# A block of cluster attention, token mixer and feed-forward: the value product in narrower column tiles, the weight conversions laid elsewhere in the queues

## The chip, the cores and the metric

The kernel runs on one core of one Trainium2 chip. What is measured is the device time of one execution in microseconds, the median of several runs. Names used below: PE is TensorE (matrix products), DVE is VectorE, ACT is ScalarE, POOL is GpSimd, SP is the engine whose queue issues the loads and stores.

## The reference

What is computed, with B = 2 batches, 8 heads, 768 tokens, 64 dimensions a head, 512 channels:

```python
q_assign = np.argmax(np.einsum('bhsd,hcd->bhsc', q_n, c_n), axis=-1)   # 16 clusters
k_assign = np.argmax(np.einsum('bhsd,hcd->bhsc', k_n, c_n), axis=-1)
mask = q_assign[:, :, :, None] == k_assign[:, :, None, :]
scores = np.where(mask, scale * np.matmul(q, k.transpose(0, 1, 3, 2)), -1000000000.0)
attn = softmax(scores)                                # rows, 1e-9 added to the sum
x = np.matmul(attn, v)                                # heads side by side: (B, S, 512)

theta = x @ w_theta                                   # token mixer
y = w_tok_r @ (x * cos(theta)) + w_tok_i @ (x * sin(theta))
x = x + y
x = x + np.maximum(x @ w_ch, 0.0)                     # channel mix

u = x + ((x.transpose(0, 2, 1) @ U) @ V).transpose(0, 2, 1)   # rank 32 over tokens
out = u + np.maximum(u @ w_ch1, 0.0) @ w_ch2          # feed-forward, 2048 wide
```

(The softmax is written out in the reference; the last three products are float32 too.)

## The kernel before

Everything works on tiles of 128 partitions. The order of each engine's instructions is the order in which the program is written (a manual schedule); an engine whose next instruction waits holds up all behind it.

**Products in parts.** A float32 operand is often split into a high part (rounded, written by ACT: `wh`, `xh`, `uh`, `z`, `gh`) and a low part (the rest, written by POOL or DVE: `wl`, `xl`, `ul`, `gl`). A product is then three passes: high with high, high with low, low with high (`PASSES`).

**Attention.** Eight groups g, each two heads of one batch. A group has six steps p. In each step PE computes a pair of key tiles' scores for one head (`scores_pair`, L301), ACT their exponentials `p` (L306); PE also computes the next group's row maxima (`max_pair`, L249). The value product `pv` (L314) is queued by pairs of key tile kt and half of the queries hf, and taken off in the odd steps, four pairs at a time. In step 5, and in step 1 of the next group, the row sums (`sum_keys`, L333) stand directly ahead of such a value block; they multiply with a block of ones into four tiles of 32 columns. After each step `fill` gives a number of units of other work to DVE, ACT and POOL: first the queue `bg`, then pieces of conversions.

**Conversions.** The weights are stored in 64 bits and have to be turned into float32. One `Convert` covers 768 columns: load 768 KB into one of two stage buffers `st`, then `magnitude` (ACT, L382, tile `cv`), `bits` (DVE, L386), `top` (DVE, L390), `low` (DVE, L394), then the high part `wh` (ACT, L399) and the low part `wl` (POOL, L403). `conv_step` issues the next piece; after `low` it puts the two last ones into `conv_after` and starts the next load (`conv_start` loads only while fewer than two conversions are in work). `conv_until` and `wcol` issue all pieces that are still missing when PE's program comes to a product that needs the tile. The order of the conversions is one queue: w_theta, then w_tok_r and w_tok_i by turns, then w_ch, then w_ch1 (`w1`) and w_ch2 (`w2`) with U and V (`ub`, `vs`) among them.

**Token mixer.** 24 steps (u, st), 26 with the lead of two. Step n computes theta on PE (L476, L480), then a chain ACT L483, DVE L484 and L485, ACT L486 to L488, DVE L493, ACT L496 gives z = x cos, x sin in high parts; the low parts are L502, the first on DVE, the second on POOL. `ymix` (L518) for step n - 2 follows on PE: 24 matrix products of 384 columns. Three `conv_step` stand in each step, except that steps 16 to 19 have one. From step 20, POOL computes `xl` (`split_x`, L463) for the channel mix.

**Channel mix to feed-forward.** `chmix(b, e)` (L536, 24 products of 384 columns) writes x back with two additions on DVE (L541); `turn` transposes it in four pieces (L552). `low1` (L588) and `low2` (L608, additions L610) are the rank-32 part. `split_u` (L615, L616) makes `uh` and `ul`. Then 48 pairs (c, f) of the feed-forward: `ff1(c, f)` (L633, results `gh` L638 and `gl` L640) runs two ahead of `ff2(c, f)` (L653). ff1(c, f) uses columns 512 f to 512 f + 511 of w1's row of tiles, so f = 0 lies in its first tile of 768 columns, f = 3 in the third.

Of the kernel before, what the change touches and what calls it, by code (L numbers as in the profile page):

```python
# [10 lines left out]
F32 = mybir.dt.float32  # L11
# [9 lines left out]
B, H, S, D, C = 2, 8, 768, 64, 16  # L21
DM, RANK, DFF = 512, 32, 2048
P = 128
# [17 lines left out]
def tile_cluster_block(ctx: ExitStack, tc: tile.TileContext, qk, v, cent, wth, wr, wi, wch,  # L41
# [9 lines left out]
    def slot(name, dt=F32, shape=None):  # L51
        return sp.tile(shape or [P, S], dt, tag="slot", name=name)
# [57 lines left out]
    def cols(hf):  # L110
        return slice(hf * HALF, (hf + 1) * HALF)
# [198 lines left out]
    def pv(g, kt, hf):  # L310
        if kt == 0 and hf == 0:
            pvt[g] = banks("pv", "pv")
        for h in range(2):
            nc.tensor.matmul(out=pvt[g][hf][64 * h:64 * h + 64, :HALF], lhsT=v_t[g][:, kt, 64 * h:64 * h + 64],  # L314
                             rhs=pt[g, h, kt][:, hf * HALF:(hf + 1) * HALF],
                             start=(kt == 0), stop=(kt == NT - 1))

    def pv_out(g):
# [235 lines left out]
    ub = []  # L554
    vs = []

    def keep_u0(c):
        for i in range(4):
            t = slot(f"ub{i}", F32, [P, 6, P])
            nc.gpsimd.memset(t, 0.0)  # L560
            ub.append(t)

    def keep_u(c, g):
        z = c.t.rearrange("p (k r) -> p k r", r=RANK)
# [130 lines left out]
    def attention():  # L695
# [12 lines left out]
        for g in range(NG):  # L708
# [13 lines left out]
            if g == 2:  # L722
                tok = [c for p in zip(weigh_in(wr, NT * S, wr_t), weigh_in(wi, NT * S, wi_t)) for c in p]
                conv_load.extend(tok[:6])
                late = tok[6:]
            if g == 6:
                conv_load.extend(late)
# [5 lines left out]
            for p in range(NT):  # L733
# [24 lines left out]
                if g > 0 and p == 5:  # L758
                    bg.appendleft((.95, lambda: norm_x(g - 1)))
                    bg.appendleft((.97, lambda: spread(g - 1)))  # L760
                fill(1.7 if nxt else 3.4)
                if g > 0 and p == 1:
                    max_rows(g, 1)
                if nxt and p == 3:
# [105 lines left out]
    def mixer():  # L870
# [4 lines left out]
        for n in range(len(seq) + LEAD):  # L875
            if n < len(seq):
                theta(*seq[n])
                conv_step()
                theta_z(*seq[n])
            if n >= LEAD:  # L880
                ymix(*seq[n - LEAD])
            if n == 1:
                row_sums(last)
            if n == 2:
                spread(last)
                norm_x(last)
            if n not in range(16, 20):
                conv_step()
            if n < len(seq):
                theta_lo(*seq[n])  # L890
            if n not in range(16, 20):
                conv_step(1)
            if n in (9, 10):
                for t in range(2):
                    split_x(1, 2 * (n - 9) + t)
            if n == 12:
                conv_load.extend(weigh_in(wch, NP * DM, wch_t))
                c1, c2 = weigh_in(w1, NF * DM, w1_t), weigh_in(w2, NF * DM, w2_t)
                conv_load.extend([c1[0], c2[0]])
                conv_load.append(Convert(u_in, S, 0, [keep_u0] + [lambda c, g=g: keep_u(c, g) for g in range(4)], 32, 4))  # L900
                conv_load.append(Convert(v_in, S, 0, [keep_v, keep_vl], 32))
                for p in zip(c1[1:], c2[1:]):
                    conv_load.extend(p)
                conv_start()
            if 20 <= n <= 23:
                split_x(0, n - 20, nc.gpsimd)
            if n in (24, 25):
                split_x(1, n - 24, nc.gpsimd)

        for e in range(NP):  # L910
            chmix(0, e)
            if e in (0, 1):
                split_x(1, 2 + e)
            turn(0, e)
            conv_step()
        conv_until(uv, "u")
        conv_until(uv, "v")
        chmix(1, 0)
        turn(1, 0)
        low1(0)  # L920
        conv_step()
        chmix(1, 1)
        turn(1, 1)
        conv_step()
        low2(0, 0)
        low2(0, 1)
        split_u(0, 0)
# [82 lines left out]
```

## Time and profile before

| what | value |
|---|---|
| median of 3 runs (lowest to highest) | 720.88 us (719.17 to 721.48) |
| the profiled execution | 724.71 us, span 722.9 us |
| TensorE (PE) busy | 695.8 us, 96% of the span |
| VectorE (DVE), ScalarE (ACT), GpSimd (POOL) busy | 435.8, 300.9, 198.0 us |
| mean granted TensorE clock | 0.986 |

The span is the time from the first to the last instruction of the profiled execution. Attention ends at about 254.7 us of it, the mixer at 404.3, the feed-forward begins at 444.4. A granted clock of 1.00 is TensorE's full speed. Time in which an engine that is not the bottleneck stands idle costs nothing, so what counts is what PE waits for, and in which stage.

### The profile page before, as it was taken

The numbers are of one execution on the slowest core, as the hardware profiler recorded it, in microseconds if no ns is written. First come the engines' busy times: TensorE is split into PE (matmuls) and PEld (weight loads), VectorE is DVE, ScalarE is ACT, GpSimd is POOL, SyncE is SP. The second block draws the span as 40 slices with busy tenths as digits, with TensorE's granted clock in tenths as the row PEclk, the third lists the DMA queues.
The fourth block names the chain that finished last, engine by engine and source line by source line (L and its number), as shares of the span: only waits on it lengthen the run. The fifth ranks groups of instructions, "written<-read, shape, count | busy, mean of one in ns | idle before, by whom it ended". The sixth has DMA issues, their size and how long they took to land.

```text
span 722.9 us, 10608 instructions
## 1 busy us (share of the span) xinstructions
PE 695.8 (96%) x4109; PEld 550.2 (76%) x4110; DVE 435.8 (60%) x746; ACT 300.9 (42%) x613; POOL 198.0 (27%) x191
## 2 busy tenths in 40 slices
PE   7689998999999999999996999999999999999997
PEld 3455554665655499999995999898888888888986
DVE  5786996888898553448587877635344453332222
ACT  5654754665677634445464612422222222110000
POOL 9603224144155521113254712321221211100000
PEclk9899999999999999999999899999999999999999
DMA  7968667576422500002122211022122221100112
GB/s 216 224 141 246 175 154 200 168 178 155 127 88 88 175 1 1 2 1 73 44 55 88 88 44 44 0 88 88 45 87 58 74 87 30 30 1 0 59 40 77
DMA packets 21506, 64.05 MB, mean 89 GB/s; under 512 B 4272, under 2 KB 6192, under 8 KB 21456
## 3 DMA queue, kind: packets, MB, share of 16 engines
q1 hardware_dynamic: 21456, 63.37, 30.6%
q8 instruction: 32, 0.52, 0.3%
q14 instruction: 18, 0.15, 0.1%
HBM read 40.94 MB, written 3.15 MB: 61 GB/s over the span
## 4 chain that ended last, share of the span: by engine, by line
PE 84%; DVE 8%; ACT 4%; DMA 2%; issue 1%; SPq 0%; DVEq 0%; ACTq 0%
PE g L633 19%; PE acc L653 18%; PE y L518 11%; PE st L301 8%; PE pv L314 8%; PE h L536 5%; PE l L333 4%; PE th L476 4%; PE smax L249 4%; DVE mx L253 3%; PE h L588 1%; DMA st<-in_wr_dram 1%; DVE tht L484 1%; PE sims L119 1%; ACT p L306 1%
## 5 line engine op out<-in xcount | busy, mean ns | idle before, releaser
L403 POOL TENSOR_TENSOR wl<-cv,wh 128x768 fp32r<-128x768 f32 (+1 forms) x40 | 80.3, 2008 | 228.5 <-ACT wh L399 171.8
L640 DVE SCALAR_TENSOR_TENSOR gl<-g,gh 128x512 fp32r<-128x512 f32 x48 | 33.2, 692 | 155.7 <-ACT gh L638 155.7
L638 ACT ACTIVATE gh<-g 128x512 fp32r<-128x512 f32 x48 | 28.7, 598 | 202.1 <-PE g L633 202.1
L253 DVE TENSOR_REDUCE mx<-smax 128x1 f32<-128x512 f32 x144 | 90.1, 681 | 29.8 <-PE smax L249 29.5
L518 PE MATMUL y<-wh,z 128*128 128x384 f32 x384 | 89.9, 346 | 6.9 <-ACT z L496 6.9
L306 ACT ACTIVATE p<-st 128x512 f32<-128x512 f32 x192 | 79.2, 505 | 33.6 <-PE st L301 27.0
L633 PE MATMUL g<-uh,wh 128*128 128x512 f32 (+1 forms) x256 | 87.0, 340 | 0.0
L633 PE MATMUL g<-uh,wl 128*128 128x512 f32 (+1 forms) x256 | 86.6, 338 | 0.0
L633 PE MATMUL g<-ul,wh 128*128 128x512 f32 (+1 forms) x256 | 86.2, 337 | 0.0
L301 PE MATMUL st<-qp,kp 128*128 128x256 f32 (+1 forms) x384 | 80.8, 354 | 1.1 <-ACT p L306 1.1
L653 PE MATMUL acc<-gh,wh 128*128 128x512 f32 x192 | 76.0, 396 | 0.0
L653 PE MATMUL acc<-gh,wl 128*128 128x512 f32 x192 | 75.6, 394 | 0.0
L653 PE MATMUL acc<-gl,wh 128*128 128x512 f32 x192 | 75.4, 393 | 0.0
L518 PEld LDWEIGHTS y<-wh,z 128*128 128x128 f32 x384 | 68.2, 192 | 7.8 <-ACT z L496 7.7
L301 PEld LDWEIGHTS st<-qp,kp 128*128 128x128 f32 x384 | 58.2, 194 | 19.1 <-issue 6.1
L314 PE MATMUL pv<-p,v 128*64 128x384 f32 x384 | 67.7, 496 | 2.2 <-ACT p L306 2.1
L314 PEld LDWEIGHTS pv<-p,v 128*64 128x64 f32 x384 | 25.5, 137 | 40.3 <-issue 33.4
L633 PEld LDWEIGHTS g<-ul,wh 128*128 128x128 f32 x256 | 48.5, 190 | 6.5 <-POOL ul L616 0.4
L633 PEld LDWEIGHTS g<-uh,wl 128*128 128x128 f32 x256 | 48.5, 189 | 5.7
L633 PEld LDWEIGHTS g<-uh,wh 128*128 128x128 f32 x256 | 48.4, 189 | 5.6
L518 PE MATMUL y<-wl,z 128*128 128x384 f32 x192 | 49.7, 340 | 0.0
L502 POOL TENSOR_TENSOR z<-tht,z 128x256 fp32r<-128x256 f32 x24 | 19.7, 821 | 94.8 <-ACT z L496 94.7
(129 smaller groups left out, 1206.4 us busy)
## 6 DMA issues: line engine op xcount, KB each, us to landing
st<-in_w_dram SPq DMA_DIRECT2D x20, 768.0 KB, 4.2
raw<-in_qk_dram SPq DMA_DIRECT2D x16, 384.0 KB, 5.3
qp<-hi SPq DMA_DIRECT2D x30, 192.0 KB, 2.9
st<-in_wr_dram SPq DMA_DIRECT2D x6, 768.0 KB, 4.5
st<-in_wi_dram SPq DMA_DIRECT2D x6, 768.0 KB, 4.3
kp<-hi SPq DMA_DIRECT2D x32, 96.0 KB, 2.9
qp<-lo SPq DMA_DIRECT2D x32, 96.0 KB, 2.7
v<-in_v_dram SPq DMA_DIRECT2D x8, 384.0 KB, 4.9
```

The costliest lines, as they stand in the source:

```text
L249: nc.tensor.matmul(out=ps[:, c:c + w], lhsT=qp[s, h, 0][:, (a + j) * P:(a + j + 1) * P], rhs=kp[s, h, 0][:, k0:k0 + w], start=True, stop=True)
L253: nc.vector.tensor_reduce(mx_t[g, h][:, o:o + n], ps.rearrange("p (n w) -> p n w", n=n), axis=AX.X, op=ALU.max)
L301: nc.tensor.matmul(out=ps[:, c:c + n], lhsT=kp[s, h, w][:, (a + j) * P:(a + j + 1) * P], rhs=qp[s, h, w][:, q0:q0 + n], start=(w == 0), st ...
L306: nc.scalar.activation(out=pt[g, h, a + j][:, q0:q0 + n], in_=ps[:, c:c + n], func=AF.Exp, scale=float(D) ** -0.5)
L314: nc.tensor.matmul(out=pvt[g][hf][64 * h:64 * h + 64, :HALF], lhsT=v_t[g][:, kt, 64 * h:64 * h + 64], rhs=pt[g, h, kt][:, hf * HALF:(hf + ...
L333: nc.tensor.matmul(out=ps[o:o + 32, :HALF], lhsT=ones, rhs=pt[g, h, kt][:, cols(hf)], start=(kt == 3 * a), stop=(kt == 3 * a + 2))
L403: nc.gpsimd.tensor_tensor(t[:, :c.w], c.t, f32(c.hi[:, :c.w]), op=ALU.subtract)
L518: nc.tensor.matmul(out=yps[u, j][hf][:, :HALF], lhsT=lhs, rhs=w[st][e][:, hf * HALF:(hf + 1) * HALF], start=(st == 0 and n == 0), stop=(st ...
L536: nc.tensor.matmul(out=ps[hf][:, :HALF], lhsT=wv[a], rhs=xs[b, t][c][:, hf * HALF:(hf + 1) * HALF], start=(n == 0), stop=(n == 11))
L633: nc.tensor.matmul(out=ps[:, o:o + w], lhsT=wv[a], rhs=us[b, t][e][:, s0:s0 + w], start=(n == 0), stop=(n == 11))
L640: nc.vector.scalar_tensor_tensor(gl, ps, 0.0, f32(gh), op0=ALU.max, op1=ALU.subtract)
L653: nc.tensor.matmul(out=aps[c, e], lhsT=wv[a], rhs=g[x], start=(first and i == 0), stop=(last and i == 2))
```

## The change

The value product is written in four tiles of 32 columns for each (kt, hf), in place of two of 64. The loads are asked for as soon as the first token weights are queued in group 2. In group 7, `fill` gets 2.0 units a step in place of 3.4. In the mixer, steps 16 and later have no conversion pieces; `split_x(0, .)` goes from POOL to DVE; the clearing of `ub` goes from U's conversion to steps 13 to 16, one tile each. w1 and w2 come after U and V in the queue. In the channel mix three pieces, and later two, stand where one stood.

```diff
@@ -310,9 +310,9 @@
     def pv(g, kt, hf):
         if kt == 0 and hf == 0:
             pvt[g] = banks("pv", "pv")
-        for h in range(2):
-            nc.tensor.matmul(out=pvt[g][hf][64 * h:64 * h + 64, :HALF], lhsT=v_t[g][:, kt, 64 * h:64 * h + 64],
-                             rhs=pt[g, h, kt][:, hf * HALF:(hf + 1) * HALF],
+        for r in range(0, P, 32):
+            nc.tensor.matmul(out=pvt[g][hf][r:r + 32, :HALF], lhsT=v_t[g][:, kt, r:r + 32],
+                             rhs=pt[g, r // 64, kt][:, cols(hf)],
                              start=(kt == 0), stop=(kt == NT - 1))
 
     def pv_out(g):
@@ -554,11 +554,10 @@
     ub = []
     vs = []
 
-    def keep_u0(c):
-        for i in range(4):
-            t = slot(f"ub{i}", F32, [P, 6, P])
-            nc.gpsimd.memset(t, 0.0)
-            ub.append(t)
+    def clear_u(i):
+        t = slot(f"ub{i}", F32, [P, 6, P])
+        nc.gpsimd.memset(t, 0.0)
+        ub.append(t)
 
     def keep_u(c, g):
         z = c.t.rearrange("p (k r) -> p k r", r=RANK)
@@ -722,6 +721,7 @@
             if g == 2:
                 tok = [c for p in zip(weigh_in(wr, NT * S, wr_t), weigh_in(wi, NT * S, wi_t)) for c in p]
                 conv_load.extend(tok[:6])
+                conv_start()
                 late = tok[6:]
             if g == 6:
                 conv_load.extend(late)
@@ -758,7 +758,7 @@
                 if g > 0 and p == 5:
                     bg.appendleft((.95, lambda: norm_x(g - 1)))
                     bg.appendleft((.97, lambda: spread(g - 1)))
-                fill(1.7 if nxt else 3.4)
+                fill(1.7 if nxt else 2.)
                 if g > 0 and p == 1:
                     max_rows(g, 1)
                 if nxt and p == 3:
@@ -875,7 +875,8 @@
         for n in range(len(seq) + LEAD):
             if n < len(seq):
                 theta(*seq[n])
-                conv_step()
+                if n < 16:
+                    conv_step()
                 theta_z(*seq[n])
             if n >= LEAD:
                 ymix(*seq[n - LEAD])
@@ -884,26 +885,27 @@
             if n == 2:
                 spread(last)
                 norm_x(last)
-            if n not in range(16, 20):
+            if n < 16:
                 conv_step()
             if n < len(seq):
                 theta_lo(*seq[n])
-            if n not in range(16, 20):
-                conv_step(1)
+            if n < 16:
+                conv_step()
             if n in (9, 10):
                 for t in range(2):
                     split_x(1, 2 * (n - 9) + t)
             if n == 12:
                 conv_load.extend(weigh_in(wch, NP * DM, wch_t))
                 c1, c2 = weigh_in(w1, NF * DM, w1_t), weigh_in(w2, NF * DM, w2_t)
-                conv_load.extend([c1[0], c2[0]])
-                conv_load.append(Convert(u_in, S, 0, [keep_u0] + [lambda c, g=g: keep_u(c, g) for g in range(4)], 32, 4))
+                conv_load.append(Convert(u_in, S, 0, [lambda c, g=g: keep_u(c, g) for g in range(4)], 32, 4))
                 conv_load.append(Convert(v_in, S, 0, [keep_v, keep_vl], 32))
-                for p in zip(c1[1:], c2[1:]):
+                for p in zip(c1, c2):
                     conv_load.extend(p)
                 conv_start()
+            if 13 <= n <= 16:
+                clear_u(n - 13)
             if 20 <= n <= 23:
-                split_x(0, n - 20, nc.gpsimd)
+                split_x(0, n - 20)
             if n in (24, 25):
                 split_x(1, n - 24, nc.gpsimd)
 
@@ -912,16 +914,16 @@
             if e in (0, 1):
                 split_x(1, 2 + e)
             turn(0, e)
-            conv_step()
+            conv_step(3)
         conv_until(uv, "u")
         conv_until(uv, "v")
         chmix(1, 0)
         turn(1, 0)
         low1(0)
-        conv_step()
+        conv_step(2)
         chmix(1, 1)
         turn(1, 1)
-        conv_step()
+        conv_step(2)
         low2(0, 0)
         low2(0, 1)
         split_u(0, 0)
```

DVE at the start of the feed-forward. `ul12` is the low part of u for the second batch's third tile, `cv_4675` and `cv_4980` (before) are w1's and w2's fourth tiles, `cv_4877` (changed) w1's third tile and `cv_5134` w2's third; `gl` are the feed-forward's low parts. Before:

```order
L616 TENSOR_TENSOR ul12_4936<-xT6_2850,uh12_4935 128x768
L640 SCALAR_TENSOR_TENSOR gl_4974<-g_4959,gh_4972 128x512
L390 SCALAR_TENSOR_TENSOR cv_4675<-st_4532,cv_4675 128x768
L394 SCALAR_TENSOR_TENSOR cv_4675<-st_4532,cv_4675 128x768
L640 SCALAR_TENSOR_TENSOR gl_5023<-g_4996,gh_5021 128x512
L386 TENSOR_SCALAR cv_4980<-cv_4980 128x768
```

Changed:

```order
L615 TENSOR_TENSOR ul12_5103<-xT6_3006,uh12_5102 128x768
L386 TENSOR_SCALAR cv_4877<-cv_4877 128x768
L390 SCALAR_TENSOR_TENSOR cv_4877<-st_4836,cv_4877 128x768
L394 SCALAR_TENSOR_TENSOR cv_4877<-st_4836,cv_4877 128x768
L386 TENSOR_SCALAR cv_5134<-cv_5134 128x768
L390 SCALAR_TENSOR_TENSOR cv_5134<-st_4879,cv_5134 128x768
L639 SCALAR_TENSOR_TENSOR gl_5158<-g_5126,gh_5156 128x512
```

All three pieces of w1's third tile now stand between `ul12` and the low part `gl_5158` of the result of ff1(0,3), which reads that tile; before, it had been converted in the channel mix.

POOL at the mixer's start. `z` are the low parts of x sin of the first steps, `rl` the last group's reciprocal row sums, `wl` low parts of token weights. Before:

```order
L403 TENSOR_TENSOR wl_2882<-cv_2854,wh_2880 128x768
L502 TENSOR_TENSOR z_2989<-tht_2979,z_2989 128x256
L349 COPY rl_3023<-rl4_3020 32x12 x8
L502 TENSOR_TENSOR z_3018<-tht_3008,z_3018 128x256
L502 TENSOR_TENSOR z_3059<-tht_3049,z_3059 128x256
```

Changed:

```order
L502 TENSOR_TENSOR z_3170<-tht_3157,z_3170 128x256
L403 TENSOR_TENSOR wl_3177<-cv_3011,wh_3172 128x768
L349 COPY rl_3211<-rl4_3208 32x12 x8
L502 TENSOR_TENSOR z_3206<-tht_3195,z_3206 128x256
L403 TENSOR_TENSOR wl_3224<-cv_3165,wh_3220 128x768
L502 TENSOR_TENSOR z_3251<-tht_3241,z_3251 128x256
```

A low part of a token weight now stands ahead of the copies of `rl` and of the second step's `z`, another ahead of the third's.

DVE around turn(0,3), whose four transposes of `xT3` are the last that low1(0) waits for. `cv_4530` (before) is w2's third tile; `cv_4663` and `cv_4710` (changed) are w1's and w2's first, `vs` belongs to V. Before:

```order
L552 STREAM_TRANSPOSE xt2_4484<-xT2_1596 128x6x32
L552 STREAM_TRANSPOSE xt3_4485<-xT2_1596 128x6x32
L386 TENSOR_SCALAR cv_4530<-cv_4530 128x768
L541 SCALAR_TENSOR_TENSOR xT3_1939<-h_4569,xT3_1939 128x384
L541 SCALAR_TENSOR_TENSOR xT3_1939<-h_4570,xT3_1939 128x384
L552 STREAM_TRANSPOSE xt0_4482<-xT3_1939 128x6x32
L552 STREAM_TRANSPOSE xt1_4483<-xT3_1939 128x6x32
L552 STREAM_TRANSPOSE xt2_4484<-xT3_1939 128x6x32
L552 STREAM_TRANSPOSE xt3_4485<-xT3_1939 128x6x32
L390 SCALAR_TENSOR_TENSOR cv_4530<-st_4441,cv_4530 128x768
```

Changed:

```order
L552 STREAM_TRANSPOSE xt3_4602<-xT2_1668 128x6x32
L577 TENSOR_TENSOR vs_4672<-cv_4608,vs_4672 32x768
L394 SCALAR_TENSOR_TENSOR cv_4663<-st_4610,cv_4663 128x768
L386 TENSOR_SCALAR cv_4710<-cv_4710 128x768
L390 SCALAR_TENSOR_TENSOR cv_4710<-st_4665,cv_4710 128x768
L541 SCALAR_TENSOR_TENSOR xT3_2035<-h_4720,xT3_2035 128x384
L541 SCALAR_TENSOR_TENSOR xT3_2035<-h_4721,xT3_2035 128x384
L552 STREAM_TRANSPOSE xt0_4599<-xT3_2035 128x6x32
L552 STREAM_TRANSPOSE xt1_4600<-xT3_2035 128x6x32
L552 STREAM_TRANSPOSE xt2_4601<-xT3_2035 128x6x32
L552 STREAM_TRANSPOSE xt3_4602<-xT3_2035 128x6x32
L394 SCALAR_TENSOR_TENSOR cv_4710<-st_4665,cv_4710 128x768
```

Where one piece stood between two turns, there are now three, and the low part of V.

## Rows read from the trace of the kernel before

**Rows 1.** The page: busy time, share of the span and instructions of each engine.

```profile
PE 695.8 (96%) x4109; PEld 550.2 (76%) x4110; DVE 435.8 (60%) x746; ACT 300.9 (42%) x613; POOL 198.0 (27%) x191
```

**Rows 2.** Windows: us, length, busy time of PE, PEld, DVE, ACT, POOL; clock, DMA, GB/s.

```profile
112.40:115.90 3.50, 3.50 (x13) 2.09 (x10) 0.84 (x1) 0.79 (x2) 1.70 (x1) 0.51 0.84 316
...
270.00:360.00 90.00, 90.00 (x593) 90.00 (x592) 47.61 (x89) 43.40 (x107) 18.05 (x19) 1.00 0.08 24
...
360.00:405.00 45.00, 38.43 (x225) 37.70 (x224) 36.44 (x43) 27.46 (x61) 22.02 (x16) 0.92 0.25 75
...
395.70:402.60 6.90, 5.01 (x16) 5.01 (x17) 4.70 (x7) 6.77 (x16) 1.69 (x2) 0.51 0.37 113
```

**Rows 3.** Chain of waits in the attention: start us, us, engine, result, line, instructions.

```profile
120.20 2.07 PE l L333 x24
...
122.27 2.73 PE pv L314 x16
...
244.69 7.89 PE pv L314 x48
```

**Rows 4.** Timeline of PE, group 7: start, us, instruction, idle before and releaser.

```profile
239.73 1.77 PE L301 MATMUL st<-qp,kp 128*128 128x512 f32 x8 [1.11 <-ACT p L306]
...
241.87 2.82 PE L333 MATMUL l<-p,ones 128*32 128x384 f32 x24 [0.38 <-ACT xT L321]
```

**Rows 5.** Timeline of ACT, group 7.

```profile
238.30 0.90 ACT L382 ACTIVATE cv<-st 128x768 f32<-128x768 f32 x1 [3.44 <-DMA st<-in_wr_dram]
```

**Rows 6.** Timelines of POOL and PE at the mixer's start.

```profile
266.30 0.74 POOL L502 TENSOR_TENSOR z<-tht,z 128x256 fp32r<-128x256 f32 x1
...
266.00 0.59 PE L518 MATMUL y<-wh,z 128*128 128x384 f32 x2
```

**Rows 7.** Chain of waits at the mixer's end and in the channel mix.

```profile
397.59 6.72 PE y L518 x24
...
404.31 20.82 PE h L536 x120
```

**Rows 8.** Timelines of DVE and POOL in the mixer's last steps.

```profile
380.78 4.64 DVE L484 TENSOR_SCALAR tht<-tht 128x256 f32<-128x256 f32 x1
...
382.50 2.78 POOL L560 MEMSET ub<- 128x768 f32 x4
```

**Rows 9.** Timeline of DVE in the channel mix.

```profile
403.13 2.06 DVE L525 TENSOR_TENSOR xT<-y,xT 128x384 f32<-128x384 f32 x4
...
405.11 2.45 DVE L394 SCALAR_TENSOR_TENSOR cv<-st,cv 128x768 int32<-128x768 int32 x1
...
421.65 1.01 DVE L541 SCALAR_TENSOR_TENSOR xT<-h,xT 128x384 f32<-128x384 f32 x2
...
422.58 1.14 DVE L552 STREAM_TRANSPOSE xt<-xT 128x192 f32<-128x192 f32 x4
...
443.79 0.96 DVE L616 TENSOR_TENSOR ul<-xT,uh 128x768 fp32r<-128x768 f32 x1
```

**Rows 10.** Chain of waits at the feed-forward's start.

```profile
462.40 2.77 PE g L633 x12
```

**Rows 11.** Timeline of DVE at the feed-forward's start.

```profile
462.65 0.96 DVE L616 TENSOR_TENSOR ul<-xT,uh 128x768 fp32r<-128x768 f32 x1
...
466.45 1.65 DVE L390 SCALAR_TENSOR_TENSOR cv<-st,cv 128x768 int32<-128x768 int32 x1
...
468.14 0.96 DVE L394 SCALAR_TENSOR_TENSOR cv<-st,cv 128x768 int32<-128x768 int32 x1
...
472.15 0.55 DVE L386 TENSOR_SCALAR cv<-cv 128x768 int32<-128x768 int32 x1
```

**Rows 12.** Timeline of POOL at the feed-forward's start.

```profile
463.62 1.84 POOL L616 TENSOR_TENSOR ul<-xT,uh 128x768 fp32r<-128x768 f32 x1 [2.09 <-ACT uh L615]
...
465.42 1.86 POOL L403 TENSOR_TENSOR wl<-cv,wh 128x768 fp32r<-128x768 f32 x1
```

**Rows 13.** Timeline of ACT at the feed-forward's start.

```profile
471.40 0.84 ACT L399 ACTIVATE wh<-cv 128x768 fp32r<-128x768 f32 x1
```

## The prediction

> **What bounds the kernel now.** I read the shares first: TensorE (PE) is busy for 695.8 us of a span of 722.9 us [rows 1], so every gain must come out of the 27 us in which it stands idle, or out of passes that it runs too slowly. Next come the windows: from 270 to 360 us PE is busy for 90.00 of 90.00 us, though every step of the token mixer there has conversion pieces beside it; from 360 to 405 us it is busy for 38.43 of 45.00 us, and in 395.70 to 402.60 us the granted clock is 0.51 [rows 2]. That is the lower of its two levels, 1.2 GHz for 2.4. Then the chain of waits and the timelines say what PE waits for. Three places matter: group 7 of the attention, the mixer's last steps, and the passage from the channel mix into the feed-forward, where PE hardly waits at present.
>
> **The change part by part.** All costs are set against the profiled execution (724.71 us, span 722.9). It lies 3.83 us above the median of the three runs, 720.88; I carry the difference over to the median.
>
> *The value product.* One pair (kt, hf) is now two passes of two 64-column tiles each; it becomes two passes of four 32-column tiles each. The same shape is there already in the row sums: 24 instructions, six passes, take 2.07 us, 0.345 a pass; 16 value instructions, eight passes, take 2.73 us, 0.341 a pass [rows 3]. So a pass of four narrow tiles is no faster than one of two wide ones. What can go is the step from one tile shape to the other. The last value block, 24 passes in a row, takes 7.89 us, 0.329 a pass [rows 3]; by this 2.73 us hold 0.10 us beyond the eight passes. A value block follows row sums directly at 15 places: 15 x 0.10 = **-1.5 us**. Bounds: -1.9, were it 0.125 each, and +0.7, were each of the 192 passes to take the 0.004 us more that separates 0.345 from 0.341.
>
> The Trainium skill, "TensorEngine Tiling (Array Packing)", section Theoretical Speedup, gives up to 2x for a free dimension of up to 64 and up to 4x for up to 32; by it the change would halve the value blocks. Rival D takes this up.
>
> *The added start of loads in group 2.* It finds two conversions already loaded and does nothing: the queue that issues loads (SP) reads alike through the attention in both orders. The wait for a token-weight load in that group, with the slow clock behind it at 112.4 us [rows 2], stays. **0.**
>
> *Less filling in group 7.* Two token-weight conversions fewer lie in the last group. There ScalarE (ACT) stood 3.44 us before a load [rows 5] while the exponentials queued behind it; PE waited 1.11 and 0.38 us, and the row sums took 2.82 instead of 2.07 us [rows 3, 4]. The changed order has the conversion that waited one step later, when its load has had that much longer. 1.11 + 0.38 + 0.75 = **-2.2 us** (bounds 0, if the later conversion waits as long, and -2.2).
>
> *The two conversions in the mixer's first steps.* They now lie in the chain of theta(0) and theta(1). On VectorE (DVE) a 0.55 us and a 0.95 us piece stand ahead of theta(1)'s first operation; a third, 0.96, lies where DVE waits for ACT's sines anyway. On GpSimd (POOL) a low half of 1.85 us stands ahead of eight copies and of z's low half. That low half ran from 266.30 for 0.74 us, and y(1), begun at 266.00, reads it after ten of its 24 instructions, at 266.00 + 10/24 x 4.16 = 267.73 [rows 6]: 0.69 us of slack. Alone, 1.5 us on DVE cost 1.5 - 0.69 = 0.8 us. If one DVE operation must also wait for the 1.85 us on POOL, 2.65. I take **+1.7 us** in the middle.
>
> *No conversions after step 15, clearing of ub spread, split_x on DVE.* Between 360 and 405 us PE idles for 45.00 - 38.43 = 6.57 us [rows 2]. The last y takes 6.72 us [rows 7] where 24 instructions of the same width take 20.82 / 5 = 4.16: 2.55 us for the low clock after the longest wait. What PE waits for is DVE and ACT: one operation on DVE, 0.30 us alone, took 4.64 us while POOL went from a split to four clearings without a break [rows 8]. All of these leave the place. From 270 to 360 us PE never waits with more work beside it [rows 2], so I give the whole back: 6.57 + 2.55 = **-9.1 us** (bounds -6.6, the idle time alone, and -9.1).
>
> *What these steps did must be done elsewhere.* Channel weight tile 2 is finished on demand in chmix(0,0): its low half on POOL comes about when the fourth quarter wants it, **+0.3 us** (0 to 0.7).
>
> Then the channel mix. In the order, DVE goes from the mixer's last additions (2.06 us, begun at 403.13, 1.2 us ahead of chmix [rows 7, 9]) through four pairs of additions of 1.01, four turns of 1.14, two splits of 0.96 [rows 9, 11], a small one that I put at 0.7, a narrower piece of about 0.64 (two thirds of 0.96), three rounds of 0.55 + 0.95 + 0.96 and a last 0.55 + 0.95 [rows 11], to the end of turn(0,3). This sums to 22.8 us (2.06 + 4.04 + 4.56 + 1.92 + 0.7 + 0.64 + 7.38 + 1.5), so it ends 21.6 us after chmix begins. low1(0) wants it 20.82 us [rows 7] + 0.3 after that. Before, the same turn ended at 422.58 + 1.14 = 423.72 [rows 9] and low1 began at 404.31 + 20.82 = 425.13: 1.4 us of slack become -0.5. And pieces there run long beside POOL: one took 2.45 us that takes 0.96 alone [rows 9, 11], 1.5 more. Bounds 0.5, with no piece hit, and 5.0, with three; I take one: **+2.0 us**. Behind it ff1(0,0) wants ul02, which was ready at 443.79 + 0.96 = 444.75 [rows 9], hardly in time. Two more pieces, 0.95 + 0.96, stand ahead of it on DVE: **+1.5 us** (0 to 1.9).
>
> *The first feed-forward tiles.* This is the largest cost. ff1(0,3) reads the third tile of w1. Before, that tile was ready, and ff1(0,3) began at 462.40 without a wait [rows 10]. In the changed order its conversion is forced at that point: DVE does its three pieces behind ul12, ACT its high half, POOL its low half, and PE stands. I lay this on the rows of before. ul12 ends on DVE at 462.65 + 0.96 = 463.61; the first piece, 0.55, ends at 464.16. POOL is in ul13 to 463.62 + 1.84 = 465.46, and a low half of w2 follows at once, 1.85, to 467.31 [rows 11, 12]. Before, a piece that is 0.95 alone took 1.65 us at 466.45 and ended when POOL's 1.86 us did, give or take 0.95 [rows 11, 12]; and the operation of 4.64 us got no turn between POOL's instructions [rows 8]. So the second piece runs from 467.31 to 468.26, the third to 469.22, the high half, 0.84 [rows 13], to 470.1: 7.7 us after 462.40. The low half is done 1.85 later, at 471.95; PE wants it two instructions after the high half, 0.46 us: 1.4 more. **+9.1 us.** Were POOL no hindrance, the three pieces would end at 466.07, the high half at 466.95: 4.55 + 1.4 = 5.95 us. These are the bounds (9.1 and 5.95); the rows are nearer to the first.
>
> The Trainium skill, "SBUF — State Buffer", section SBUF: two separate sides, speaks against this change: DVE and GpSimd share a pair of ports that one instruction locks to its end, where DVE has two operands in SBUF and GpSimd reads SBUF. The long rows on DVE agree with it. By it the wait is the 9.1 us, without it 5.95.
>
> *The clock after a new wait.* After a wait of PE the granted clock was 0.51 for 3.50 us in group 2 [rows 2], which cost 3.50 x 0.49 = 1.7 us, and 2.55 us at the last y, as above. After the wait in the feed-forward I take **+2.5 us** (0 to 5, as other new waits may do it or none).
>
> Sum: -1.5 - 2.2 + 1.7 - 9.1 + 0.3 + 2.0 + 1.5 + 9.1 + 2.5 = **+4.3 us**, from 724.71 to 729.0 for a profiled execution and from 720.88 to **725.2 us** for the median.
>
> **The rivals.** *A, the pieces are not held up by POOL.* For: alone, the same pieces take 0.95 to 0.96 [rows 11]. Against: the rows of 1.65, 2.45 and 4.64 [rows 8, 9, 11]. Then the wait in the feed-forward is 5.95 (3.15 less), the mixer's first steps cost 0.8 (0.9 less) and low1 0.5 (1.5 less): 4.3 - 5.55 = -1.2, about 719.6, no change. *B, faster: the moved pieces fall into idle time of DVE.* Beside what A says, the mixer's first steps, chmix, low1 and ff1(0,0) then cost nothing; the forced conversion alone is left, 5.95 and the lower price of the clock, 1.7: -1.5 - 2.2 - 9.1 + 5.95 + 1.7 = -5.1, 715.7. It decides as soon as DVE ends turn(0,3) half a microsecond earlier than I lay it, and ul02 two. For: DVE is busy for 36.44 of the 45 us to 405 [rows 2], and loses several long rows there. Against: the sum of 22.8 us has no idle time in it. *C, dearer:* the port holds up low1 by the full 5.0 us, and a second wait costs the clock (5.0 in all): +3.0 + 2.5, 730.7. *D, a narrow tile's pass takes half the time:* 192 passes x 0.341 / 2 = -32.7 us, 688 to 693. The rows of the same tile shape speak against it [rows 3]. *E, the change doesn't do what it says:* so it is for the loads in group 2, at no price; the rest is in the order.
>
> **How the numbers follow.** About 0.3% (2.2 us) is what a measurement of this kernel can tell from no change: faster is below 718.7, slower above 723.0. Forecast 0.53 (722 to 729, nearly all of it slower), A 0.21, B 0.13, C 0.11, D 0.02. A little of the forecast and of B falls into no change: faster 0.16, same 0.24, slower 0.60. The range goes from 716.0, which takes in A and the dearer part of B, to 730.0, which leaves out most of C: with D, about 0.2 are outside.
>
> **What would show it.** In the changed kernel's profile: row sums and value blocks keep 0.33 to 0.345 a pass, with value blocks after row sums at some 2.6 us; no wait for p in group 7; a wait of 1 to 3 us for z's low half (POOL) within the first two y; hardly a wait from 340 us to the channel mix, with the clock at 1.00; a wait of PE of about 8 us for the high half of w1 (ACT) ahead of ff1(0,3), and a slow clock behind it. If that wait is missing or below 5 us, or if value blocks take half the time, I am wrong, and the kernel is faster.

## The result

The changed kernel takes 724.56 us (median of 6 runs, 723.73 to 726.07), the kernel before in the same six rounds 720.16 us (719.04 to 721.48): 1.0064 times the time before, 95% interval 1.0045 to 1.0082. That is slower, by 4.4 us; the forecast was 4.3 us more, 725.2 us. The profiled execution took 723.99 us with a span of 722.2.

What PE waits for in the changed kernel, longest first (what waits, for whom: us in all, how often, the longest; "..." stands for lines left out):

```profile
PE g L632 <- ACT wh L399: 7.6, 1, 7.6
...
PE h L587 <- DVE xt L552: 1.3, 1, 1.3
...
PE g L632 <- POOL wl L403: 1.0, 1, 1.0
...
PE y L518 <- POOL z L502: 1.0, 1, 1.0
PE y L518 <- ACT z L496: 0.8, 2, 0.5
PE g L632 <- POOL ul L615: 0.8, 1, 0.8
```

Of these six the profile before has only the fifth, with 6.9 us there. The first is the wait for w1's third tile ahead of ff1(0,3).

I lay the two profiles side by side at points that PE's program has in both: the first and the fifth theta, the first product of chmix, low1(0), low1(1) and the first ff2 behind ff1(0,3). The third column is a second profile of the kernel before (experiment 1). A column says how long PE took from the point before to this one.

| stretch of PE's program | before, first profile | before, second | changed | change against the first | against the second | forecast |
|---|---|---|---|---|---|---|
| start to the mixer's first theta | 254.66 | 253.33 | 246.67 | -8.0 | -6.7 | -3.7 |
| to the fifth theta | 15.58 | 15.60 | 17.56 | +2.0 | +2.0 | +1.7 |
| to chmix(0,0) | 134.07 | 131.89 | 124.56 | -9.5 | -7.3 | -9.1 |
| to low1(0) | 20.82 | 20.82 | 22.84 | +2.0 | +2.0 | +2.3 |
| to low1(1) | 22.28 | 22.28 | 23.84 | +1.6 | +1.6 | +1.5 |
| to the ff2 behind ff1(0,3) | 17.76 | 17.76 | 28.99 | +11.2 | +11.2 | +11.6 |
| to the end of the span | 257.73 | 257.72 | 257.74 | 0 | 0 | 0 |
| span | 722.9 | 719.4 | 722.2 | -0.7 | +2.8 | +4.3 |

(The forecast of 2.3 is 0.3 + 2.0, that of 11.6 is 9.1 + 2.5.)

In the attention, value blocks behind row sums and elsewhere, and the last block, by the chain of waits (start, us, engine, line, instructions), beside [rows 3]:

```profile
119.22 2.58 PE pv L314 x32
...
126.35 2.72 PE pv L314 x32
...
234.93 2.07 PE l L333 x24
237.00 7.74 PE pv L314 x96
244.74 1.94 PE l L333 x24
```

A block behind row sums takes 2.58 for 2.73 us, one elsewhere 2.72. The row sums of group 7 are back at 2.07, and PE's waits of [rows 4] are gone; of ACT's 3.44 us before a load [rows 5] 1.12 are left, and PE doesn't feel them.

The mixer's last steps, and the stretch of slow clock behind the wait in the feed-forward, as windows (columns as in [rows 2]):

```profile
356.00:400.00 44.00, 43.68 (x271) 43.36 (x270) 23.98 (x45) 19.70 (x45) 9.18 (x8) 1.00 0.06 15
458.00:463.60 5.60, 4.53 (x10) 3.13 (x11) 0.57 (x1) 0.00 (x0) 2.17 (x1) 0.50 0.43 140
```

In the last steps PE idles for 0.3 of 44 us where it had idled for 6.6 of 45, and the clock is at 1.00 throughout. The price stands at 458 us. There the timelines of DVE, POOL, ACT and PE read, beside [rows 10 to 13]:

```profile
450.72 0.96 DVE L615 TENSOR_TENSOR ul<-xT,uh 128x768 fp32r<-128x768 f32 x1
451.60 0.55 DVE L386 TENSOR_SCALAR cv<-cv 128x768 int32<-128x768 int32 x1
452.18 2.45 DVE L390 SCALAR_TENSOR_TENSOR cv<-st,cv 128x768 int32<-128x768 int32 x1
454.67 2.44 DVE L394 SCALAR_TENSOR_TENSOR cv<-st,cv 128x768 int32<-128x768 int32 x1
...
451.75 2.07 POOL L615 TENSOR_TENSOR ul<-xT,uh 128x768 fp32r<-128x768 f32 x1 [2.14 <-ACT uh L614]
453.78 2.52 POOL L403 TENSOR_TENSOR wl<-cv,wh 128x768 fp32r<-128x768 f32 x1
458.06 2.17 POOL L403 TENSOR_TENSOR wl<-cv,wh 128x768 fp32r<-128x768 f32 x1 [1.77 <-ACT wh L399]
...
457.14 0.84 ACT L399 ACTIVATE wh<-cv 128x768 fp32r<-128x768 f32 x1 [3.95 <-DVE cv L394]
...
458.04 0.79 PE L632 MATMUL g<-uh,wh 128*128 128x512 f32 x1 [7.57 <-ACT wh L399]
...
460.29 0.79 PE L632 MATMUL g<-uh,wl 128*128 128x512 f32 x1 [1.03 <-POOL wl L403]
```

ul12 ends on DVE at 451.68. DVE's second piece, L390, is held until POOL's ul13 ends at 453.82; POOL's next is held in turn until that piece ends at 454.63; the third piece, L394, until POOL ends at 456.30. Then comes the high half, and PE starts 7.57 us late; two products on, it stands 1.03 us for the low half.

### The profile page after: what moved, and what is told of

It reads as the page before. It is cut to its first block, busy times and chain, and to the rows that moved or that the text cites. A ratio compares the mean times of both kernels' runs of the same rounds, so it can differ in the third digit from the quotient of the medians.

```text
span 722.2 us, 11389 instructions
## 1 busy us (share of the span) xinstructions
PE 690.6 (96%) x4494; PEld 547.5 (76%) x4494; DVE 427.0 (59%) x750; ACT 303.2 (42%) x613; POOL 183.6 (25%) x187
## 4 chain that ended last, share of the span: by engine, by line
PE 79%; DVE 8%; ACT 4%; POOL 3%; issue 2%; DMA 2%; SPq 1%; POOLq 0%; ACTq 0%; DVEq 0%
PE g L632 18%; PE acc L652 18%; PE y L518 11%; PE st L301 8%; PE pv L314 8%; PE th L476 4%; PE l L333 4%; PE smax L249 4%; DVE mx L253 2%; PE h L587 2%; DVE xT L609 1%; DMA qp<-lo 1%; POOL wl L403 1%; DVE xt L552 1%; ACT p L306 1%
## 5 line engine op out<-in xcount | busy, mean ns | idle before, releaser
L403 POOL TENSOR_TENSOR wl<-cv,wh 128x768 fp32r<-128x768 f32 (+1 forms) x40 | 77.0, 1925 | 256.7 <-ACT wh L399 207.8
L518 PE MATMUL y<-wh,z 128*128 128x384 f32 x384 | 87.8, 341 | 1.8 <-POOL z L502 1.0
L314 PE MATMUL pv<-p,v 128*32 128x384 f32 x768 | 66.3, 487 | 2.2 <-ACT p L306 2.1
L314 PEld LDWEIGHTS pv<-p,v 128*32 128x32 f32 x768 | 24.1, 110 | 38.8 <-issue 35.1
L249 PE MATMUL smax<-kp,qp 128*128 128x512 f32 x192 | 43.8, 349 | 2.3 <-POOL kp L208 1.3
```

What stands on the lines that cost most here:

```text
L249: nc.tensor.matmul(out=ps[:, c:c + w], lhsT=qp[s, h, 0][:, (a + j) * P:(a + j + 1) * P], rhs=kp[s, h, 0][:, k0:k0 + w], start=True, stop=True)
L314: nc.tensor.matmul(out=pvt[g][hf][r:r + 32, :HALF], lhsT=v_t[g][:, kt, r:r + 32], rhs=pt[g, r // 64, kt][:, cols(hf)], start=(kt == 0), st ...
L403: nc.gpsimd.tensor_tensor(t[:, :c.w], c.t, f32(c.hi[:, :c.w]), op=ALU.subtract)
L518: nc.tensor.matmul(out=yps[u, j][hf][:, :HALF], lhsT=lhs, rhs=w[st][e][:, hf * HALF:(hf + 1) * HALF], start=(st == 0 and n == 0), stop=(st ...
```

## The experiments

Each is the changed kernel with one edit, unless said otherwise. Ratios are to the kernel before, run in turns with it.

**1. The kernel before again.**

> The kernel before, unchanged. The two profiled executions differ by 0.7 us (724.71 before, 723.99 changed), the medians by 4.4 us (720.16 and 724.56). Theory: the first profile of the kernel before holds stretches at the low clock that most executions don't have (3.5 us in group 2, 1.6 to 1.7 us lost; perhaps the last y's 2.55 us too). Then this one takes 719 to 721.5 us, its mean clock lies above 0.986, and one or both of these stretches are gone from the profile. Rival: the stretches are in every execution, and the profiled execution is longer for another reason: then the clock is 0.986 again and both stretches stand in the profile.

722.14 us (10 runs, 719.09 to 724.35), ratio 1.0014 (0.999 to 1.0038), as it must be, and a little above the 719 to 721.5 us expected. The profiled execution took 721.19 us, mean clock 0.988. The value block behind the wait in group 2, and the chain at the mixer's end:

```profile
111.33 2.16 PE L314 MATMUL pv<-p,v 128*64 128x384 f32 x12 [1.95 <-ACT p L306]
...
379.54 1.86 DVE tht L484
...
393.59 7.23 PE y L518 x24
```

The slow clock in group 2 is gone (2.16 us; 2.82 in the first profile), that of the last y is not. So the theory holds by half. The other 2.2 us of the 3.5 between the profiles lie in the mixer's last steps, whose waits for ACT's z were 6.9 us in the first and 4.5 in the second. The operation on DVE beside the clearing of ub, 4.64 us long in [rows 8], takes 1.9 here (1.86 in the chain): it ended just behind POOL's split, ahead of the clearings, and PE's wait of 1.72 us at 388.26 in the first profile is missing here. So that row, from which the prediction explained these waits, is one of those that differ from execution to execution.

**2. Wide value tiles.**

```diff
-        for r in range(0, P, 32):
...
+        for h in range(2):          # two tiles of 64 columns, as before
...
```

> The changed kernel with the value product in two 64-column tiles again. Theory (a pass of four narrow tiles costs as much as one of two wide ones; only the change of shape behind the row sums is saved): 1.5 to 2.6 us more than the changed kernel, some 726 to 727, value blocks behind row sums 2.73 us again. Rival (narrow tiles stream twice as fast): some 30 us more, 755. Rival (they save nothing): 724.6.

727.77 us, ratio 1.0106 (1.0075 to 1.0136): 3.2 us more than the changed kernel's median, 3.0 by the ratios. Narrow tiles gain, a little more than I had allowed; nothing like half of the value blocks' time. Blocks behind row sums are at 2.73 us again. In its profile the first theta comes 4.6 us later than in the changed kernel's; some 1.6 of these are the clock, which fell in group 2:

```profile
121.47 2.73 PE pv L314 x16
...
111.60:115.10 3.50, 3.50 (x13) 2.06 (x10) 0.93 (x1) 0.80 (x2) 1.77 (x1) 0.51 0.84 312
```

**3. A piece in each of the mixer's last steps.**

```diff
             if n < len(seq):
                 theta_lo(*seq[n])
-            if n < 16:
-                conv_step()
+            conv_step()
```

> The changed kernel with one conversion piece in each of the mixer's steps 16 to 25, ten in all; nothing else moved. Theory: the third tile of w1 is then ready before ff1(0,3), so PE's waits of 7.57 and 1.03 us there and the slow clock behind them (2.6) go, 11.2 us in all, and at most 1 to 3 us come back as waits of the mixer's last steps: 713 to 717 us. Rival (the mixer's last steps wait as they did in the kernel before, 6.6 us idle and more): 718 to 722.

715.71 us, ratio 0.9926 (0.9906 to 0.9946): 9 us less than the changed kernel's median (10 by the ratios), and faster than both kernels. PE no longer waits ahead of ff1(0,3), and it doesn't wait in the last steps either. What came back stands at low1(0):

```profile
412.38 7.25 PE L587 MATMUL h<-xt,ub 128*128 128x128 f32 x48 [2.55 <-DVE xt L552]
```

A wait of 2.55 us, and 7.25 us for products that take 5.36: the clock again. The theory holds; its "1 to 3 us back" came at another place than I had said.

**4. Full filling in group 7.**

```diff
-                fill(1.7 if nxt else 2.)
+                fill(1.7 if nxt else 3.4)
```

> The changed kernel with 3.4 units of filling a step in group 7, as in the kernel before. Theory: the waits of 1.11 and 0.38 us and the row sums of 2.82 us come back (+2.2), the mixer's first steps lose theirs (-2.0): within 1 us of the changed kernel, 724 to 725.5. Rival (the mixer's first steps wait anyway, for PE's own lead): +2.2, 726.8. Rival (group 7 waits anyway): -2.0, 722.5.

726.54 us, ratio 1.0085 (1.0054 to 1.0116): 2.0 us more by the medians, 1.5 by the ratios. That is above the theory's 724 to 725.5. PE waits in group 7 again:

```profile
234.95 1.76 PE L301 MATMUL st<-qp,kp 128*128 128x512 f32 x8 [1.10 <-ACT p L306]
```

From the row sums in group 6's step 1 to the first theta PE takes 52.29 us for 49.48 (+2.8; waits of 1.10 and 0.39 us again), and the mixer's first steps lose their 2.0 us (15.57 from the first theta to the fifth). So by place the two offset each other but for 0.8 us, as the theory has it, and the rival that the first steps wait anyway falls, though its time (+2.2) came nearer. The rest of the 1.9 us between the two profiles is the clock: behind the wait ahead of ff1(0,3) it stays low for longer here and costs 1.1 us more than in the changed kernel's profile.

**5. The mixer's last steps as before.**

```diff
-                if n < 16:
-                    conv_step()
+                conv_step()
...
-            if n < 16:              # twice
+            if n not in range(16, 20):
...
-                split_x(0, n - 20)
+                split_x(0, n - 20, nc.gpsimd)
```

> The changed kernel with the mixer's last steps as in the kernel before: three conversion pieces a step (one in steps 16 to 19), the next tiles' low parts on POOL; the clearing of ub stays spread. Theory (the same work costs about as much in either place): the waits of 6.6 us and the slow clock of 2.55 us in the last steps come back in part (+5 to +9), the waits ahead of ff1(0,3) and their slow clock go (-11.2): 718 to 722 us, 3 to 6 us less than the changed kernel. Rival (the last steps waited for the clearing of ub alone): they stay without waits, 712 to 715. Rival (the wait ahead of ff1(0,3) is not the missing tile's): 729 or more.

725.42 us, ratio 1.0065 (1.0042 to 1.0089): no better than the changed kernel, 3 us above what the theory allowed. PE's timeline:

```profile
381.09 0.61 PE L518 MATMUL y<-wh,z 128*128 128x384 f32 x2 [0.25 <-ACT z L496]
...
383.49 0.96 PE L518 MATMUL y<-wh,z 128*128 128x384 f32 x4 [1.43 <-DVE z L502]
...
389.54 0.62 PE L518 MATMUL y<-wh,z 128*128 128x384 f32 x2 [2.31 <-ACT z L496]
...
391.93 1.22 PE L518 MATMUL y<-wh,z 128*128 128x384 f32 x4 [1.43 <-DVE z L502]
...
422.21 3.14 PE L587 MATMUL h<-xt,ub 128*128 128x128 f32 x17 [4.15 <-DVE xt L552]
```

The first part came as expected: 5.4 us of waits in the last steps and a slow clock behind them (8.0 us more from the fifth theta to chmix), and no wait at ff1(0,3). What I had left out is low1(0): 4.15 us of wait and the slow clock behind it, since three pieces behind each chmix now fall together with the low parts that POOL makes of them. DVE and POOL there:

```profile
403.01 1.98 DVE L463 TENSOR_TENSOR xl<-xT,xh 128x768 fp32r<-128x768 f32 x1 [0.63 <-ACT xh L461]
...
417.49 1.36 DVE L390 SCALAR_TENSOR_TENSOR cv<-st,cv 128x768 int32<-128x768 int32 x1
...
402.32 1.85 POOL L463 TENSOR_TENSOR xl<-xT,xh 128x768 fp32r<-128x768 f32 x1 [2.71 <-ACT xh L461]
...
416.18 1.85 POOL L403 TENSOR_TENSOR wl<-cv,wh 128x768 fp32r<-128x768 f32 x1 [4.80 <-ACT wh L399]
```

A split of 0.96 us takes 1.98 while POOL works, a piece of 0.95 takes 1.36. Clearing ub was not the only reason for the waits in the last steps: it is spread here too, and they are back.

**6. POOL kept off the forced conversion.**

```diff
-        (nc.gpsimd if t % 2 else nc.vector).tensor_tensor(lo, ...)
+        (nc.gpsimd if t % 2 and (b, t) != (1, 3) else nc.vector).tensor_tensor(lo, ...)
...
         turn(1, 3)
+        while conv_after:
+            conv_after.popleft()()
```

> The changed kernel with POOL kept free while the third tile of w1 is converted: w2's second tile gets its parts ahead of ff1(0,0), and ul13's low part is made on DVE (0.96 us more on DVE ahead of the pieces). Theory (POOL's two instructions held up DVE's second and third piece by 1.5 us each): pieces of 0.95 and 0.96 us, PE's wait for wh falls from 7.57 to 5.5 us, all in all 2 us less, 722.5. Rival (DVE's pieces are long for another reason, or DVE's own queue is all that counts): the wait grows by the 0.96 us to 8.5, 725.5.

722.97 us, ratio 1.0029 (1.0013 to 1.0045): 1.6 us less by the medians, 2.5 by the ratios. DVE does more work ahead of the pieces, and PE waits 2 us less:

```profile
451.15 1.90 DVE L615 TENSOR_TENSOR ul<-xT,uh 128x768 fp32r<-128x768 f32 x2
452.97 0.55 DVE L386 TENSOR_SCALAR cv<-cv 128x768 int32<-128x768 int32 x1
453.55 0.96 DVE L390 SCALAR_TENSOR_TENSOR cv<-st,cv 128x768 int32<-128x768 int32 x1
454.55 0.96 DVE L394 SCALAR_TENSOR_TENSOR cv<-st,cv 128x768 int32<-128x768 int32 x1
...
456.44 0.79 PE L632 MATMUL g<-uh,wh 128*128 128x512 f32 x1 [5.58 <-ACT wh L399]
...
458.69 0.79 PE L632 MATMUL g<-uh,wl 128*128 128x512 f32 x1 [1.03 <-POOL wl L403]
```

2.45 and 2.44 us became 0.96 and 0.96. This is the test of the port: the rival would have had 8.5 us of wait.

**7. No pieces in the mixer's first two steps.**

```diff
-                if n < 16:          # three times
+                if 2 <= n < 16:
```

> The changed kernel without conversion pieces in the mixer's steps 0 and 1; the two last token weights are then finished in steps 2 to 4, two steps ahead of their use. Theory: PE's waits for z in the first two y (1.0 and 0.8 us, 2.0 us against the kernel before) go: 722.5 us. Rival (they come back later, as y for the last token tiles waits): 724.5.

723.11 us, ratio 1.0029 (1.0016 to 1.0043): 1.5 us less by the medians, 2.5 by the ratios. The fifth theta comes 15.7 us behind the first, as before the change (17.56 with it), and nothing waits later for the token weights. That was the theory.

**8. The later weights queued earlier.** As 7, and:

```diff
-            if n == 12:
+            if n == 7:
...
-            if 13 <= n <= 16:
-                clear_u(n - 13)
+            if 5 <= n <= 8:
+                clear_u(n - 5)
...
-            conv_step(3)
+            conv_step(1 + e // 2)
```

> The changed kernel without pieces in steps 0 and 1, with the channel and feed-forward weights queued in step 7 in place of 12 and ub cleared in steps 5 to 8, so that the pieces which found nothing to do between the token weights' end and step 12 are used; one or two pieces in place of three behind each chmix of the first batch. Theory: nothing is converted late, so the waits ahead of ff1(0,3) with their clock go (-11.2), the mixer's first steps (-2.0), low1's and ul's (-1 to -2): 709 to 711 us, faster than both kernels. Rival (the mixer's middle steps, which have 90.00 of 90 us now, begin to wait when pieces fill them all): 713 or more.

710.12 us (709.75 to 711.37), ratio 0.9857 (0.9832 to 0.9881): 10 us less than the kernel before, 14 less than the changed one. Windows from the fifth theta to chmix and from there into the feed-forward, and the chain behind:

```profile
262.00:388.00 126.00, 125.67 (x810) 124.65 (x809) 87.45 (x135) 69.66 (x169) 37.13 (x34) 1.00 0.15 44
388.00:440.00 52.00, 51.17 (x320) 49.30 (x319) 37.14 (x77) 14.10 (x23) 9.20 (x5) 1.00 0.19 61
...
388.09 20.80 PE h L536 x120
...
447.48 2.77 PE g L632 x12
```

chmix to low1(0) takes 20.80 us, without a wait, ff1(0,3) starts behind ff2(0,0) without one, and the mixer's middle steps carry the additional pieces: PE is busy for 125.67 of 126 us. They are not quite free: from the fifth theta to chmix it takes 126.0 us for 124.6 in the changed kernel, though hardly any of it is idle. The added waits for z in the first two y are gone too; PE's 0.8 us for ul ahead of low1(1) are still there.

**9 and 10. Narrow tiles alone, in the kernel before; wide tiles in the changed one again.**

> The kernel before with nothing but the value product in four 32-column tiles. The pair of the changed kernel with and without it differed by 3.2 us in the medians, while the value blocks in the two profiles account for 2.8 (15 places at 0.15, the block of 48 pairs of passes 0.15, the last row sums 0.13, and some tenths). Theory: 2.5 to 3.2 us less than the kernel before. Second question, the low clock behind the wait of 2 us in group 2: it stood in two of three profiles with wide tiles and in none of seven with narrow ones. If it belongs to the wide tiles, this profile has the value block behind that wait at 2.14 to 2.16 us and the gain is up to 1.6 us larger in the mean; if it comes by chance, it may stand here too, with 2.8.

> The changed kernel with wide value tiles once more, for one more profile of the wait in group 2. If the low clock belongs to wide tiles, the value block behind the wait takes 2.8 to 2.9 us again; if by chance, 2.2 as in the second profile of the kernel before or 2.8, and the time lies 1.6 us lower without it: 726 to 728 with, 724.5 to 726.5 without.

Narrow tiles alone: 718.13 us, ratio 0.9959 (0.9935 to 0.9983), 2 to 3 us less, about as the theory has it (2.5 to 3.2). And the value blocks behind the wait of 2 us in group 2, narrow in the kernel before and wide in the changed one:

```profile
110.00 3.68 PE L314 MATMUL pv<-p,v 128*32 128x384 f32 x24 [1.99 <-ACT p L306]
...
110.30 2.16 PE L314 MATMUL pv<-p,v 128*64 128x384 f32 x12 [1.87 <-ACT p L306]
```

Here the narrow one is slow and the wide one is not, at waits of 1.99 and 1.87 us. So the low clock there doesn't belong to a tile's width. Of twelve profiles it stood in three; all twelve have this wait, of 1.87 to 2.32 us. The mean clock of each execution is on record: of 65 of the kernel before, run in turns with the experiments, 13 have 0.986 or less, as its first profile has, and of the 12 with narrow tiles alone 5 have 0.983, as the one profiled; where the clock fell in those without a profile is not known. The wide tiles took 727.15 us in their single execution, more than the 724.5 to 726.5 expected without the low clock; the first theta comes 3.1 us later than in the changed kernel's profile.

## Why the prediction was right, and where it was not

**The forced conversion (+9.1 and +2.5, measured 8.6 and 2.6).** Right in place, chain and size: 7.57 + 1.03 us of wait, and the rest of the 11.2 us is the low clock behind it (in other runs with the same wait it cost up to 1.1 us more, as in experiment 4). The upper bound, with POOL in the way, was the one to take; experiment 6 shows the lower one (5.58 us of wait against 4.55 + 0.96 for the split moved to DVE), experiment 3 shows that the tile is the cause. One detail was wrong: POOL doesn't keep its turn, the two engines take turns, which comes to the same sum here. The prediction had taken it from the row of 4.64 us [rows 8], which the second profile doesn't have. The Trainium skill, "SBUF — State Buffer", section SBUF: two separate sides, says that whichever of the two starts first holds the shared ports for its whole instruction; the trace agrees (both long pieces end 0.81 us behind POOL's instruction, less than the 0.96 that they take alone). The condition quoted in the prediction, two operands on DVE and a POOL that reads, fits these pieces but not the 4.64 us that it counts among its long rows: that operation (L484) has one operand, and clearings read nothing.

**The mixer's first steps (+1.7, measured +2.0).** Right, and by the mechanism of the upper bound: L390 and L484 on DVE and a low half on POOL, each held up by the other.

```profile
252.53 1.50 DVE L390 SCALAR_TENSOR_TENSOR cv<-st,cv 128x768 int32<-128x768 int32 x1
253.94 1.94 DVE L484 TENSOR_SCALAR tht<-tht 128x256 f32<-128x256 f32 x1
...
253.17 2.56 POOL L403 TENSOR_TENSOR wl<-cv,wh 128x768 fp32r<-128x768 f32 x1
...
260.90 0.73 POOL L502 TENSOR_TENSOR z<-tht,z 128x256 fp32r<-128x256 f32 x1
```

L484, 1.94 us here, takes 0.29 alone. Experiment 7 takes the pieces out of these steps and the 2 us go.

**The mixer's last steps (-9.1, measured -9.5 against the profile that I had, -7.3 against the second).** The way was right, the base was not. "I carry the difference over to the median" was the step that failed: 3.8 us of the profiled execution lay above the median, and I didn't ask where. Against the second profile 2.2 us lay in these waits (the DVE operation of 4.64 us takes 1.9 there) and 1.6 in a low clock in group 2. Part of the argument was wrong as well: that every step of the mixer up to 360 us has pieces beside it. The token weights are done before step 3, and nothing else is queued before step 12 (in the trace of before, DVE has no piece between 246 and 329 us), so most of the window of 90.00 us showed only that steps without pieces don't wait. That was all the term needed, but it hid the idle steps that experiment 8 uses.

**Low1(0) and ff1(0,0) (+2.3 and +1.5, measured +2.0 and +1.6).** The sizes were right, the mechanism of the first was not. I had let POOL hit one piece by 1.5 us. In the changed kernel no piece there is held up, but DVE begins later and waits twice:

```profile
388.81 1.02 DVE L525 TENSOR_TENSOR xT<-y,xT 128x384 f32<-128x384 f32 x2 [1.06 <-PE y L518]
...
393.57 1.02 DVE L541 SCALAR_TENSOR_TENSOR xT<-h,xT 128x384 f32<-128x384 f32 x2 [1.68 <-PE h L536]
...
400.56 0.96 DVE L463 TENSOR_TENSOR xl<-xT,xh 128x768 fp32r<-128x768 f32 x1 [0.82 <-ACT xh L461]
...
411.12 1.15 DVE L552 STREAM_TRANSPOSE xt<-xT 128x192 f32<-128x192 f32 x4
```

The last additions start with the last y's end, not 1.2 us ahead of it: [rows 9] had them early because that y was slow. Then DVE waits 1.68 us for chmix's product and 0.82 for ACT's high part; no row here is longer than alone. Nor does low1(0) wait for the end of turn(0,3), to which the prediction led its sum: it starts at 411.63, behind the first of the four transposes, while the last ends at 412.27. For ff1(0,0) the delay on DVE came as laid out, but it hit another tile: PE waits 0.80 us for the low part that POOL makes of the fourth tile, behind DVE's additions, and hardly (0.05) for ul02. Experiment 5 shows the hits that I had feared, once POOL has low parts to make at the same time.

**The attention (-3.7, measured -6.7 against the second profile).** Two terms were too small. Value tiles: -1.5 was forecast, bounds +0.7 to -1.9; experiments 2 and 9 give 2 to 3.2 us, and the rows 0.15 us for each of the 15 blocks behind row sums, 0.15 for the last block and 0.13 for the last row sums, 2.5 in all. The step that failed is the 0.10 us: I took the pace of the last block, 0.329 us a pass, as one without loss, but with narrow tiles the same passes take 7.74 / 24 = 0.3225. Group 7: -2.2 forecast, 2.8 in experiment 4. The remaining 1.4 us lies for the greater part ahead of group 2, where the profiles spread by nearly as much: the value block behind the wait begins between 108.95 and 110.15 us in those with narrow tiles and between 110.30 and 111.33 in those with wide ones.

So the time was right because the costs came out nearly exact in sum (16.8 us for 17.1), and because two errors offset each other, which is luck: the gains in the attention were 3.0 us larger than forecast, those in the mixer's last steps 1.8 us smaller in a usual execution, and between the two profiles 2.8 us are left where the medians say 4.4 (3.2 to 5.9). The other 1.6 us are where the profiles lie in their spread: that of the changed kernel 0.6 below its median, the second one of the kernel before 1.0 above the median of the first rounds. No run shows why.

**The rivals.** A (POOL no hindrance) and B (idle time on DVE) fall with experiment 6 and the table's lines, C with low1's rows, D with experiments 2 and 9. E holds for the loads in group 2: the wait there is still 2.10 us.

## What to carry to other kernels

Work that is taken out of a stage because it waits there must be followed to the point where its result is read: here ten steps without conversions gave 7 to 9 us back and a tile that came too late took 11, while steps 2 to 11 of the same loop had asked for pieces and found none queued, and queueing the weights five steps earlier gave both (710.1 us). Before a difference is carried from a profiled execution to the median, ask which of its rows are peculiar to that execution: here 3.8 us.

## What the hardware showed that I had not expected

- After waits of PE of 1.87 to 2.32 us at the same place of the program the granted clock fell to 0.51 for some 3.5 us in three of twelve profiled executions and stayed at 1.00 in nine; after longer waits (2.55, 4.15, 4.2, 5.58 and 7.57 us in the runs above) the products that followed were slow each time. Such a slow stretch costs 1.6 to 3.8 us beyond the wait (2.82 for 2.16 us and what follows it in group 2; 7.25 for 5.36; 7.23 for 4.17; most in experiment 4). What decides it after the short waits no run shows.
- A product in narrower tiles, with twice the instructions, takes as long (2.72 us for 2.73), and directly behind row sums of the same shape 0.15 us less (2.58).
- DVE and POOL hold each other up by turns, both ways: 2.45 and 2.44 us on DVE for pieces of 0.96, and 2.52 us on POOL for 1.85 between them. Who comes next is not always the same: one DVE operation took 4.64 us beside a split and four clearings of POOL in one execution, and 1.9 at the same place in another.
